# Last LayerNorm by column halves on two engines, fewer products held back, and a re-planned instruction order in a fused attention and gated-MLP kernel

## The chip, the cores and the metric

The kernel runs on one core of a Trainium2 chip. The time is device microseconds (us) from the start to the end of one execution. Engines: TensorE (PE, with its weight loads as PEld), VectorE (DVE), ScalarE (ACT), GpSimd (POOL) and SyncE (SP, which issues most of the DMAs). They run in parallel; each takes its own instructions in the order in which the program lists them, and semaphores hold an instruction until what it needs from another engine is there.

## The reference

A pre-LayerNorm block on x of 2048 rows and 512 columns, bf16:

```python
h  = x + attention(layernorm(x), wqkv, wo)           # 32 heads of 16, softmax over 2048 keys
h2 = h + mlp(layernorm(h), w_gate, w_up, w_down)     # (sigmoid(h @ w_gate) * (h @ w_up)) @ w_down, F = 1792
```

The reference returns h2.

## The kernel before

**Attention.** Scores are computed transposed: a unit is one head's 128 keys by 512 query columns (or 256 columns of two heads). Three units form a tile `pss` in PSUM; there are 683 tiles and two such buffers (`ps_s`, bufs=2), so the scores of tile n wait until tile n-2 has been read. `scores` (its matmuls are at L1119) works in four row strips of PE. For each tile ACT takes the exp of three units (1536 columns) or of two (1024 columns) at L1503. Where it takes two, DVE makes the exp of the third by integer arithmetic: `dexp_first` (L1298) writes J, and after up to four units have been gathered `dexp_rest` adds three shifted copies, the codes (L1318, 512 to 2048 columns by the number of units gathered). `av` (L1272) multiplies the probabilities, J and codes by the values and adds to one accumulator `acc`, in four column strips of PE that run side by side. `finish_group` transposes and normalises the accumulator (L1205, L1167, L1171) and writes the transposed output `ot` (L1183).

**Background work.** Projections, the LayerNorm of earlier row blocks, and the gated MLP (`ffn_up`, `ffn_down`) are generators in a queue `bg`; their matmuls (L214) are taken between score tiles. The rows are treated in eight blocks of 256; the MLP of the first seven runs in the background, that of the last one after the attention.

**The order.** At build time a planner walks through the program with a clock for each engine (`T`), a price for each operation, and picks the next instruction of the engine whose clock is lowest: `pe_step`, `act_step`, `dve_step`, `gps_step`. Prices are constants: `MM` 217.5 ns for a round of products of 512 columns, `SMM` 214 for a score tile, `S_OUT` and `S_IN` (L691) for changing PE from scores to other work and back. Due times spread the background work. Where PE has nothing to do, `fill` (L712) issues a product whose result nobody reads. `MARKS` holds one letter for each tile and engine that bends the rules at that tile: for PE it loosens the room in front of the next scores, favours background work or value products; for ACT it forbids or favours giving a unit to DVE and picks which one; for DVE it moves codes and other work before or behind J. The planner fixes the order alone; at run time only semaphores hold the engines.

**The end.** `ffn_down` of block 6 has two row tiles i of seven steps each (two of the 14 products over f at a time). Steps with f >= `FHOLD` (L1027) of the first, and all of the second, are held back (`HOLD`); the steps that aren't held go to PE before the last value products. Held steps are issued by `release(n)` (L1607), n steps at a time, between the pieces of the last block's work: two of them ahead of the last output projection (L1620, p = 3, which waits for the last `ot`), seven behind it, and the rest after the transposes. The first row tile's steps run in four column strips (L214), the second's over the whole array (L209, into `acc`). The last block's h is gathered in two PSUM tiles `hps[0]`, `hps[1]` of 128 rows and 512 columns; DVE takes the statistics (L187, L190), ACT the root (L1630), DVE the reciprocal and the scaled mean `nmr` (L1631, L1632). Then DVE normalises `hps[0]` (L1636) while ACT normalises `hps[1]` (L1638), PE transposes both (L205), DVE copies the first transpose to `hnT` (L1645), ACT the second (L1643), and the gate and up products of the last block start (L209, `gu`), 112 matmuls of 256 columns.

Of the kernel before, what the change touches and what calls it, by code (L numbers as in the profile page):

```python
# [23 lines left out]
CODE_STEP = (55, 93, 24)  # L24
MARKS = {
    "A": (
        ".....xjj.jo..xoxxooo.oo.jjoj.x.o..x..xooo.....xx.....ooo....jj.......l...j.x"
        "..oloooooooox..jj..jjjjjox..xxxxoxjlooojoj...x.lllll.ll..jx...ljooo.jjl.ll.."
        "x...ll.jj..............jjllll..j..oxll.jl...lllj.j........x.oooljj..jjjjl..."
        "jjjjj.jjjj.j..xxx.o..lllj.jjjjjjxxjj.......x.ll..l...o.x......x..o.oo...l.lo"  # L30
        "ooooooo.....lll...xo.o.oo.o.l.......olll.lox....l..x.j..l....ox.l.l........o"
        "..xjl.........jjl.jj.j...oj...xo..ooo...ool..joool..xlllloo.o.o.l.llol...jj."
        "o..oo...llll.j.l.lxl.oj.xxjjj..lll.....x.....xx....jjl.ll.jjj..ojj.....o...x"
        "x......l.......ooooo.lljljx.oj....xll.....jj.j.jj..j.jjjj.llllxl.jl..jjoo..."
        ".......oooooooojjo.xxoo.jj.jjjjj.l..ox.ll...j.l........ojjj.jjjjo.oo.x.x..."
    ),
    "P": (
        ".......ff...vRR.ww........vww..p..a..RRR....p......v.a.vaafffa.wpa....a...ww"
        "wwwwwfvvaa.vpppp.vv.R.RfR.brrRr....rr.p.....ffffff.rrrr..rrpR.p....aa.a.aaav"
        "pb...RR.b.b..b.b.p...R......vrRrRw.pp.vv....vRfvrpp...........bbRR.Rva.vvr.f"  # L40
        "f.rr.......vvv....fpbr.vvvvvv.v..rpf........r.r..bb...wpww.bb.ppaaw.pRR..pf."
        "....fpp.prR.......R.ffww.pb..v..p.f......vrrrrv..www.v.v..f....vvvvvvbRR..aw"
        "wwwff.ff...vv..p............wva...wwwfRrbbvb......p........r..fvvvpva.r...aa"
        "....pv.....wpppp...p.r...vpv............aw.bbww..w...f..f.ppp.......R.R.aa.b"
        "b.f.rrrrrrrv...rw.w.www..p....a..a...aav....ff...ffr.aa....rppv.ffff.bf....."
        "vv..r....a.Rvvv.vvp.pbb.R.v.v......r........RRv..rr..rfff..a..a...vv...frrr"
    ),
    "D": (
        "...e.e...........cc....cc...ee..........c......ce.c..........c..c..........."
        ".c..s.ssssseee.e..ceeeee.ees..sseee........e.eeeeee.cee.........s..........."  # L50
        "...sc.s........c.e.....s...........ccsssss.ss...ss...........c.cc.ccc......."
        ".....c.ccscc..eee........e.c.c.........c..eee..c.ccc..ceeeeee..c.....c.....e"
        "ee.ee..c.c........e.e.....c.cc....................ece.s..............ce.scc."
        ".s......c......e.cce......c.e.e.c.ccc.e.....c.c.c.e.ee.ce...cc......c......."
        "......ccc...cccc..c....e.............ee......e...............c.......s......"
        "c............cessss..eeecc....eee.ees.e........s.s................s.c......."
        "....scccc...e.......c.......ee.c..........e.......c..ccccccs...sse.....c..."
    ),
}

# [1 line left out]
def kernel(  # L62
# [625 lines left out]
                        moved = True  # L688

    MM = 217.5  # L690
    SMM, S_OUT, S_IN = 214.0, 113.0, 97.0  # L691
    FILL = 2000.0
    SPAN = 3413.0
    FROOM = 200
# [329 lines left out]
        yield pe(0, st["pm"])  # L1024

    HOLD = Mark(None)
    FHOLD = 6  # L1027
    LEAD = 12
    FFN_DUE = (220, 295, 371, 446, 521, 597, 672)
    bg = deque()  # L1030
# [366 lines left out]
    def pe_step():  # L1397
        nonlocal credit
        t, s, e = T["P"], nxt["s"], nxt["e"]
        ready = None  # L1400
        if s < N and (s < 2 or s - 2 in ex_end):
            ready = max(ex_end.get(s - 2, -LAT) + LAT, arrived(s))
            if ready <= t + 100 * (st["mode"] != "s") + 20:
                scores(s)
                nxt["s"] += 1
                for q, p, kt, j in tiles[s]:
                    if (q, kt, j) == (NQC + NH - 1, NT - 1, 3):
                        for g in range(2 * p * (p > 1), min(2 * p + 2, FC // 2)):
# [48 lines left out]
    def act_step():  # L1457
# [59 lines left out]
    def dve_step():  # L1517
# [97 lines left out]

    for p in range(NP):
        if p == NP - 1:
            release(2)
        for i in range(HT):
            nc.tensor.matmul(hps[i], lhsT=OT[hf, p][:, i * P:(i + 1) * P], rhs=wo_sb[:, p, :],  # L1620
                             start=False, stop=(p == NP - 1))
# [6 lines left out]
    for i in range(HT):  # L1628
# [2 lines left out]
    nc.vector.reciprocal(out=rstd[:], in_=rstd[:])  # L1631
    nc.vector.scalar_tensor_tensor(out=nmr[:], in0=mv[:, :, 0], scalar=-1.0, in1=rstd[:],  # L1632
                                   op0=ALU.mult, op1=ALU.mult)
    release(7)
    hnl = [ptp.tile([P, GU, QC], BF16, name="pt")[:, 0, :] for i in range(HT)]
    nc.vector.tensor_scalar(out=hnl[0], in0=hps[0], scalar1=mv[:, 0, 0:1], scalar2=rstd[:, 0:1],  # L1636
                            op0=ALU.subtract, op1=ALU.mult)
    nc.scalar.activation(out=hnl[1], in_=hps[1], func=ACT.Identity, bias=nmr[:, 1:2],  # L1638
                         scale=rstd[:, 1:2])
    for i in range(HT):  # L1640
        pt = transpose4(gu[i], hnl[i])
        if i % 2:
            nc.scalar.copy(out=hnT[:, :, i * P:(i + 1) * P], in_=pt)  # L1643
        else:
            nc.vector.tensor_copy(out=hnT[:, :, i * P:(i + 1) * P], in_=pt)  # L1645
    release(len(bg) * FC)
    for job in held:
        job.fn()
# [54 lines left out]
```

## Time and profile before

| | us |
|---|---|
| median of 3 runs (782.69 to 783.16) | 783.05 |
| the profiled execution, own time | 784.36 |
| its span (first to last instruction) | 782.6 |
| exps (ACT, L1503) from | 21.35 |
| last exp ends | 752.51 |
| last block's gate products start | 760.80 |

PE is busy for 756.3 us of the span, ACT for 753.4, DVE for 728.6. Busy times of ACT count an instruction from when the engine took it up, so neighbours overlap; a group's mean can therefore be longer than the distance of two starts. PE's matmuls are pipelined in the same way. In a row of a group stand: line, engine, operation, output and input with shapes, count, busy time in us and mean in ns, idle time before and what ended it. In a row in order of time: start in us, length in us, the same names, the count of merged instructions, and in brackets the idle time before with what ended it. In a row of a stage: the stretch, its length, the busy time and count of each engine, the granted PE clock as a share, DMA.

### The profile page before, as it was taken

What the parts mean: (1) busy time and instruction counts of PE and PEld (TensorE: products, weight loads), DVE (VectorE), ACT (ScalarE), POOL (GpSimd) and SP (SyncE); (2) the same over time, 40 slices, a digit from 0 to 9 for tenths busy, and PEclk for the clock granted to TensorE, in tenths of its full rate; (3) what the DMA queues carried; (4) which work ended last, traced back from release to release, by engine and by line L of the source; (5) the groups of instructions that cost most, each with busy time, mean ns of one, the idle gap of its engine ahead of it and who ended that gap; (6) DMA issues with size and microseconds to landing.
All of it is one profiled execution on the core that took longest, in us unless ns stands there. A gap on an engine that the chain in (4) does not pass through costs nothing.

```text
span 782.6 us, 34120 instructions
## 1 busy us (share of the span) xinstructions
PE 756.3 (97%) x15312; PEld 374.1 (48%) x15312; DVE 728.6 (93%) x1351; ACT 753.4 (96%) x786; POOL 50.1 (6%) x124
## 2 busy tenths in 40 slices
PE   8899999999999999999999999999999999999998
PEld 7433323444455534554455434654554345544656
DVE  6999998999999999999999999999999999999952
ACT  6999999999999999999999999999999999999972
POOL 2000000000020001000100002000100010001000
PEclk9999999999999999999999999999999999999999
DMA  6403013146012320222022401221132203214510
GB/s 200 122 2 76 2 28 69 30 97 183 9 37 70 97 57 16 77 84 57 9 64 75 115 26 30 85 84 37 37 97 83 64 24 109 84 29 124 167 33 22
DMA packets 93811, 53.00 MB, mean 68 GB/s; under 512 B 21520, under 2 KB 92576, under 8 KB 93664
## 3 DMA queue, kind: packets, MB, share of 16 engines
q1 hardware_dynamic: 92848, 50.56, 23.4%
q8 instruction: 119, 1.95, 1.0%
q10 hardware_dynamic: 816, 0.26, 0.1%
q14 instruction: 28, 0.23, 0.1%
HBM read 39.52 MB, written 2.11 MB: 53 GB/s over the span
## 4 chain that ended last, share of the span: by engine, by line
PE 39%; ACT 32%; DVE 15%; issue 11%; DMA 1%; SPq 1%; POOL 0%; ACTq 0%; DVEq 0%
ACT pt L1503 31%; PE pm L214 12%; PE acc L1272 11%; PE pss L1119 11%; DVE J L1298 7%; DVE code L1318 5%; PE gu L209 2%; ACT th L983 1%; DMA code<-in_A_x_dram 1%; DVE qd L815 1%; PE hp L1673 1%; DVE hT L967 1%; DVE xs L1205 0%; PE acc L209 0%; DVE h L932 0%
## 5 line engine op out<-in xcount | busy, mean ns | idle before, releaser
L1503 ACT ACTIVATE pt<-pss 128x1024 bf16<-128x1024 f32 (+1 forms) x683 | 713.3, 1199 | 3.1 <-PE pss L1119 2.1
L1298 DVE TENSOR_SCALAR J<-pss 128x512 uint16<-128x512 f32 x507 | 337.8, 683 | 12.2 <-PE pss L1119 10.3
L1119 PE MATMUL pss<-QT,KT 32*128 32x256 bf16 (+1 forms) x3584 | 269.4, 288 | 18.6 <-ACT pt L1503 12.3
L1318 DVE TENSOR_SCALAR code<-J 128x2048 uint16<-128x2048 uint16 (+3 forms) x405 | 254.3, 662 | 0.6
L1272 PE MATMUL acc<-pt,Vaug 128*17 128x256 bf16 (+1 forms) x2689 | 229.8, 290 | 0.0
L1272 PE MATMUL acc<-code,Vaug 128*17 128x256 bf16 (+1 forms) x2685 | 199.7, 288 | 0.2
L1119 PEld LDWEIGHTS <-KT 32*128 32x128 bf16 x3584 | 87.5, 92 | 212.4 <-issue 114.1
L1272 PEld LDWEIGHTS <-Vaug 128*17 128x17 bf16 x6269 | 138.9, 90 | 102.1 <-issue 82.8
L1272 PE MATMUL acc<-J,Vaug 128*17 128x256 bf16 (+1 forms) x895 | 141.8, 288 | 0.0
L214 PE MATMUL pm<-xT,wgu 128*32 128x256 bf16 x3136 | 117.0, 274 | 0.3 <-DVE hT L967 0.2
L214 PEld LDWEIGHTS <-wgu 128*32 128x32 bf16 x3136 | 77.3, 96 | 25.2 <-issue 23.0
L214 PE MATMUL pm<-wd,hT 128*32 128x512 bf16 x728 | 54.0, 383 | 0.0
L1171 POOL TENSOR_TENSOR o<-xs,rec 128x256 bf16<-128x256 f32 x23 | 16.5, 719 | 381.7 <-DVE rec L1167 381.7
L967 DVE SCALAR_TENSOR_TENSOR hT<-th,pm 128x512 bf16<-128x512 f32 x49 | 33.3, 679 | 6.2 <-PE pm L214 3.4
L983 ACT ACTIVATE th<-pm 128x512 f32<-128x512 f32 x49 | 31.9, 651 | 0.0
L1205 DVE STREAM_TRANSPOSE xs<-acc 128x512 f32<-128x512 f32 x32 | 22.7, 710 | 5.3 <-PE acc L1272 5.1
L214 PEld LDWEIGHTS <-hT 128*32 128x32 bf16 x728 | 14.5, 95 | 17.0 <-issue 13.2
L214 PE MATMUL pm<-xT,wk_sb 128*32 128x512 bf16 x256 | 19.9, 383 | 0.0
L214 PE MATMUL pm<-xT,wq_sb 128*32 128x512 bf16 x256 | 19.1, 383 | 0.0
L214 PE MATMUL pm<-wv_sb,xT 128*32 128x448 bf16 x256 | 18.0, 356 | 0.0
L1177 POOL TENSOR_TENSOR o<-xs,rec 128x256 bf16<-128x256 f32 x8 | 5.6, 703 | 186.5 <-DVE rec L1167 186.5
L214 PE MATMUL pm<-wo_sb,ot 128*32 128x512 bf16 x224 | 17.4, 383 | 0.0
(155 smaller groups left out, 351.8 us busy)
## 6 DMA issues: line engine op xcount, KB each, us to landing
wgu<-in_B_w_gate_dram SPq DMA_DIRECT2D x49, 256.0 KB
wgu<-in_B_w_up_dram SPq DMA_DIRECT2D x49, 256.0 KB
KT<-half_neg SPq DMA_DIRECT2D x7, 512.0 KB
QT<-qd SPq DMA_DIRECT2D x28, 128.0 KB
KT<-kd SPq DMA_DIRECT2D x7, 256.0 KB
wd<-in_B_w_down_dram SPq DMA_DIRECT2D x1, 1792.0 KB
xr<-in_A_x_dram SPq DMA_DIRECT2D x14, 128.0 KB
out_dram<-ob SPq DMA_DIRECT2D x14, 128.0 KB
```

The costliest lines, as they stand in the source:

```text
L209: nc.tensor.matmul(ps, lhsT=lhsT, rhs=rhs, start=start, stop=stop)
L214: nc.tensor.matmul(ps[r, :], lhsT=lhsT[:, r], rhs=rhs, start=start, stop=stop, tile_position=(0, 32 * j), skip_group_check=True)
L815: nc.vector.tensor_tensor(out=qd[:, 0], in0=ps, in1=RQ[:] if qc else RK[:, 0], op=ALU.mult)
L967: nc.vector.scalar_tensor_tensor(out=hT[:, 2 * k:2 * k + 2, :].rearrange("p f q -> p (f q)"), in0=th[:], scalar=1.0, in1=ps, op0=ALU.add, ...
L983: nc.scalar.activation(out=th[:], in_=ps, func=ACT.Tanh, scale=0.5)
L1119: mm = nc.tensor.matmul(pss[:, ui, a * w:(a + 1) * w], lhsT=KT[hg[a]][32 * j:32 * j + 32, kt * P:(kt + 1) * P], rhs=(QT0[q] if q < NQC and ...
L1171: V.tensor_tensor(out=o2[:, 0:NB, :].rearrange("p b (a d) -> p a b d", a=2), in0=xs[:, :, 0:DH].rearrange("p (a b) d -> p a b d", a=2), in ...
L1205: j = st["acc"] = dve(630, lambda: nc.vector.transpose(out=xs[:].rearrange("p b r -> p (b r)"), in_=acc[:]), Mark(T["P"] + 175))
L1272: nc.tensor.matmul(acc[32 * j:32 * j + VW, a * w:(a + 1) * w], lhsT=Vaug[:, kt, 4 * hg[a] + j, :], rhs=un.ap[:, a * w:(a + 1) * w], start= ...
L1298: first = nc.vector.tensor_scalar(out=J[:, k, :], in0=src, scalar1=128 * SC * LOG2E, scalar2=float(CODE_BASE), op0=ALU.mult, op1=ALU.add)
L1318: nc.vector.tensor_scalar(out=c, in0=j, scalar1=CODE_STEP[i], scalar2=None, op0=ALU.add)
L1503: ex = nc.scalar.activation(out=pt[:, lo:lo + wa, :], in_=pss[:, lo:lo + wa, :], func=ACT.Exp, scale=SC)
```

## The change

Planner: the prices `S_OUT` and `S_IN` grow; six new letters for marks are understood (and two digits), and all three mark strings are replaced, so the order of all engines' instructions changes through the attention. End: `FHOLD` grows from 6 to 12, so that three more steps of the first row tile go ahead of the last value products; one held step instead of two stands ahead of the last output projection; six instead of seven behind it, now issued after the normalisation's instructions. Each of the two row tiles is normalised in halves, columns 0 to 255 on DVE and 256 to 511 on ACT; the second transpose is copied by ACT and DVE in halves.

```diff
 MARKS = {
     "A": (
-        ".....xjj.jo..xoxxooo.oo.jjoj.x.o..x..xooo.....xx.....ooo....jj.......l...j.x"
+        ".....xxj.jo..xoxxoo..oo.jjoj.uoo..ll.xooo.....xx.....oo.ooooo..t......o..j.o"
...
-    SMM, S_OUT, S_IN = 214.0, 113.0, 97.0
+    SMM, S_OUT, S_IN = 214.0, 116.5, 106.5
...
-    FHOLD = 6
+    FHOLD = 12
...
-        room = limit - t + {"w": 150, "v": -150}.get(way, 0)
-        got = [av_ready(60.0, r) for r in (1, 2, 3, 4)]
+        room = limit - t + {"w": 150, "v": -150, "W": 400}.get(way, 0)
+        got = [av_ready(60.0, r) for r in range(1, {"1": 2, "2": 3}.get(way, 5))]
...
-            if kind == "b" and (2 * MM + S_OUT * (st["mode"] == "s") <= room + (0 if credit < 8 else 500)):
+            if kind == "b" and way != "n" and (2 * MM + S_OUT * (st["mode"] == "s") <= room + (0 if credit < 8 else 500)):
...
-        if job and (start is None or job.ready() <= start + 100):
+        if job and (start is None or job.ready() <= start + {"t": 600, "u": -300}.get(mark("A", n), 100)):
...
-        if jq and sc_end[jq[0][0]] + LAT <= t + WAITJ and (half or len(first_codes) < NJB):
+        if jq and sc_end[jq[0][0]] + LAT <= t + {"w": 700, "z": 0}.get(mark("D", nxt["e"]), WAITJ) and (half or len(first_codes) < NJB):
...
         if p == NP - 1:
-            release(2)
+            release(1)
...
-    release(7)
     hnl = [ptp.tile([P, GU, QC], BF16, name="pt")[:, 0, :] for i in range(HT)]
-    nc.vector.tensor_scalar(out=hnl[0], in0=hps[0], scalar1=mv[:, 0, 0:1], scalar2=rstd[:, 0:1],
-                            op0=ALU.subtract, op1=ALU.mult)
-    nc.scalar.activation(out=hnl[1], in_=hps[1], func=ACT.Identity, bias=nmr[:, 1:2],
-                         scale=rstd[:, 1:2])
     for i in range(HT):
-        pt = transpose4(gu[i], hnl[i])
-        if i % 2:
-            nc.scalar.copy(out=hnT[:, :, i * P:(i + 1) * P], in_=pt)
-        else:
-            nc.vector.tensor_copy(out=hnT[:, :, i * P:(i + 1) * P], in_=pt)
+        nc.vector.tensor_scalar(out=hnl[i][:, 0:HQ], in0=hps[i][:, 0:HQ], scalar1=mv[:, i, 0:1],
+                                scalar2=rstd[:, i:i + 1], op0=ALU.subtract, op1=ALU.mult)
+        nc.scalar.activation(out=hnl[i][:, HQ:D], in_=hps[i][:, HQ:D], func=ACT.Identity,
+                             bias=nmr[:, i:i + 1], scale=rstd[:, i:i + 1])
+    release(6)
+    pts = [transpose4(gu[i], hnl[i]) for i in range(HT)]
+    nc.vector.tensor_copy(out=hnT[:, :, 0:P], in_=pts[0])
+    nc.scalar.copy(out=hnT[:, 0:2, P:2 * P], in_=pts[1][:, 0:2, :])
+    nc.vector.tensor_copy(out=hnT[:, 2:4, P:2 * P], in_=pts[1][:, 2:4, :])
     release(len(bg) * FC)
```

More of the change, by code (lines that the diff above doesn't have):

```diff
@@ L26 @@
     "A": (
-        ".....xjj.jo..xoxxooo.oo.jjoj.x.o..x..xooo.....xx.....ooo....jj.......l...j.x"
[L28 to L32, printed above, removed]
@@ L33 @@
-        "o..oo...llll.j.l.lxl.oj.xxjjj..lll.....x.....xx....jjl.ll.jjj..ojj.....o...x"
-        "x......l.......ooooo.lljljx.oj....xll.....jj.j.jj..j.jjjj.llllxl.jl..jjoo..."
-        ".......oooooooojjo.xxoo.jj.jjjjj.l..ox.ll...j.l........ojjj.jjjjo.oo.x.x..."
+        ".....xxj.jo..xoxxoo..oo.jjoj.uoo..ll.xooo.....xx.....oo.ooooo..t......o..j.o"
+        "..o...oooooox..jj...j........lxxxx.......j...xtll........jxo..xuooooojl.ll.."
+        "x...ll.jj.............jjj.joo..j.......jl...lllj.j........x..oojjjjjj.jjlul."
@@ new lines @@
+        "jjjjjljjjt.j..xxxoo..luuj.jjj.j...j...j....ju.uujo...o.x..u...x..o.oo...uulo"
+        "...oooo.....uul........oo.o.o....u..olll.lox....llll.j.......o..l.l.l...llll"
+        "..xol....t....jjl.jj.j...oj...xo..oxo...otlll.ll.l..xl.llouj..loolluu.uu.u.u"
+        "o..oo...llll.j.l.jooo.....jjj..llt.tjj.j......xuuujuu.u.l.j..jjj.j.jj..o...x"
+        "xuuuu..u..xx...ooooo.lljlj..xj....xll.....jj.jljj.jjjjjjj.lllllloooo.jjoo..."
+        "j..t.ttt.ooooo.jjouuuu......jjjj.l..oxloo...j.l........ojjj.jj.......x.xtt."
@@ L36 @@
     ),
     "P": (
[L38 to L43, printed above, removed]
@@ L44 @@
-        "....pv.....wpppp...p.r...vpv............aw.bbww..w...f..f.ppp.......R.R.aa.b"
-        "b.f.rrrrrrrv...rw.w.www..p....a..a...aav....ff...ffr.aa....rppv.ffff.bf....."
-        "vv..r....a.Rvvv.vvp.pbb.R.v.v......r........RRv..rr..rfff..a..a...vv...frrr"
+        ".......ff.11vRR.11..W.....vww.WWW.W.wwwwv.W.WWW1W....n.vaaf.fa.w.aaa..a.WWWW"
+        ".w.1111v.a.vrrr.rrrrWW.W..brrpr.....r.p.b...ffff1..ffw.ff...22bb.b.aappppaav"
+        "pb...RR.b.b..b.b.p.........bvrRrrw.pp.vv....vRfvwwp22222222r..b1R........Rp2"
@@ new lines @@
+        "2.22.....v.vvvw...fpbr.vvvRR.RRr.11rrr.nn.nnnnr..bppppprfp.ba.p.app.wwww..aa"
+        "....fp..prR.....f.R.ffww.pb.ava...22.....vvrrrv....1...aawRa.apv1vvvvbRR.r22"
+        "22222.ff...wv........v....n.wva...wwwfRrpbvb....2.p........rRnfvvbbna.r....."
+        ".vvv.v.v...wpbpp...p.r....pvWW.ffR.vRRRRf.1......2rr.r..f....p.......1......"
+        "b...rrwwr......r2.222222.p....n.nR.b.....2p.f.fvvvvr.aa...WWWW..f1....f....."
+        "pW.2.2.pp.ppaaaarvp.pb..R.v.v......r..2R....RRv..vr..rfff..a..a........frrr"
@@ L47 @@
     ),
     "D": (
[L49 to L54, printed above, removed]
@@ L55 @@
-        "......ccc...cccc..c....e.............ee......e...............c.......s......"
-        "c............cessss..eeecc....eee.ees.e........s.s................s.c......."
-        "....scccc...e.......c.......ee.c..........e.......c..ccccccs...sse.....c..."
+        "...e.e..wwww.........s.cc...ee..........c......sssss.........c..c.....eeww.."
+        "cc.cs.ssssseeees..ceeeee.eezzzc..c.........e.eeecce.cee.........s..........."
+        "...sc.s........c.e.....s..ss.s.....ccsssss.ss..ess.......e...c.zc.ccc......."
@@ new lines @@
+        ".....c.ccs....eee........e.c.eeeeeeee..c..eee..c.ccc..css...e..c.ww......w.e"
+        ".w.ee..c.c........e.e.....c.......................ecee.eee.e....ss...ce.scc."
+        ".s.c....w..w...e.cce...c..c.e.e.c.ccese...cc..c.c.e.ee.cw...c.......c......."
+        "....z.ceee..cccc..s....ee............ee...ss.ww.w............c..zzzzzz......"
+        "w............cessss..eeecc....eew....sw........s.s......ww........s.c..ee..."
+        "....scccc..ce.......c......ccccc..........e.......c..ccccccs...sse.....c..."
```

## The prediction

> **What bounds the kernel now.** I read the page first, then the groups by form, then stages, then single rows in order of time.
>
> ```profile
> span 782.6 us, 34120 instructions
> PE 756.3 (97%) x15312; PEld 374.1 (48%) x15312; DVE 728.6 (93%) x1351; ACT 753.4 (96%) x786; POOL 50.1 (6%) x124
> PE 39%; ACT 32%; DVE 15%; issue 11%; DMA 1%; SPq 1%; POOL 0%; ACTq 0%; DVEq 0%
> ```
>
> Three engines are over 90% busy, and the chain that ended last (third row) passes between them: no single one owns the span. Which of them sets the pace has to be read from prices. These are the groups by form, then single rows of ACT in order of time (start, length):
>
> ```profile
> L1503 ACT ACTIVATE pt<-pss 128x1024 bf16<-128x1024 f32 x508 | 495.3, 1092 | 3.0 <-PE pss L1119 2.1 <-ACT pt L1503 0.3
> L1503 ACT ACTIVATE pt<-pss 128x1536 bf16<-128x1536 f32 x175 | 253.6, 1512 | 0.1
> L983 ACT ACTIVATE th<-pm 128x512 f32<-128x512 f32 x49 | 31.9, 651 | 0.0
> ```
> ```profile
> 21.35 1.94 ACT L1503 ACTIVATE pt<-pss 128x1024 bf16<-128x1024 f32 x2 [0.94 <-PE pss L1119]
> ...
> 35.26 1.44 ACT L1503 ACTIVATE pt<-pss 128x1536 bf16<-128x1536 f32 x1
> 39.25 1.48 ACT L1503 ACTIVATE pt<-pss 128x1536 bf16<-128x1536 f32 x1
> 47.29 1.14 ACT L1503 ACTIVATE pt<-pss 128x1024 bf16<-128x1024 f32 x1
> 51.81 1.21 ACT L1503 ACTIVATE pt<-pss 128x1024 bf16<-128x1024 f32 x1
> ...
> 748.28 0.63 ACT L983 ACTIVATE th<-pm 128x512 f32<-128x512 f32 x1
> 748.77 3.74 ACT L1503 ACTIVATE pt<-pss 128x1536 bf16<-128x1536 f32 x3
> ```
>
> The means (1092 and 1512 ns) are no prices: they overlap their neighbours. The price is the distance of starts in an unbroken run. From 35.26 to 39.25 lie three exps of 1536 columns, 1.33 us each; from 47.29 to 51.81 five of 1024, 0.904 each; a tanh takes 0.49 (748.28 to 748.77). Then ACT's work is 508 x 0.904 + 175 x 1.33 + 49 x 0.49 = 459.2 + 232.8 + 24.0 = 716.0 us. It runs from 21.35 to 752.51 (748.77 + 3.74), 731.2 us. So ACT loses only **15.2 us** in the whole attention stage. A stage cannot get shorter than ACT's work; these 15.2 us are all that a better order can win there.
>
> ```profile
> 21.35:752.50 731.15, 712.38 (x14836) 340.81 (x14837) 703.34 (x1262) 728.94 (x732) 44.53 (x102) 1.00 0.24 66
> 752.50:760.80 8.30, 8.30 (x82) 3.53 (x73) 5.29 (x13) 3.24 (x7) 0.00 (x0) 1.00 0.08 22
> 760.80:782.60 21.80, 18.46 (x155) 14.96 (x153) 5.97 (x10) 6.74 (x12) 0.00 (x0) 0.98 0.08 26
> ```
>
> In this view of stages the columns are length, PE, PEld, DVE, ACT, POOL busy, granted clock. PE is busy for 97% of the first stage at full clock and DVE for 96%: ACT's lost time is scores that came late because PE or DVE was late. The second stage is the last LayerNorm and its neighbours; the third (the last gate, up and down products) keeps its instructions.
>
> **The change part by part.** *The attention stage.* The planner's numbers and marks change the order everywhere, so I count in the built programs. Scores stand in 668 separate blocks in both, so the number of switches into and out of scores stays. On ACT 506 exps of 1024 and 177 of 1536 replace 508 and 175: two units go from DVE to ACT, 2 x (1.33 - 0.904) = **+0.85 us** on the engine with the least slack. PE loses work:
>
> ```profile
> 760.80 12.39 PE L209 MATMUL gu<-xT,KT 128*128 128x256 bf16 x112
> ```
> ```profile
> L712 PE MATMUL pm<-xT 128*32 128x512 bf16 x28 | 10.8, 386 | 0.1
> L1298 DVE TENSOR_SCALAR J<-pss 128x512 uint16<-128x512 f32 x507 | 337.8, 683 | 12.2 <-PE pss L1119 10.3
> L1318 DVE TENSOR_SCALAR code<-J 128x2048 uint16<-128x2048 uint16 x360 | 239.5, 695 | 0.5
> L1318 DVE TENSOR_SCALAR code<-J 128x1536 uint16<-128x1536 uint16 x12 | 6.3, 558 | 0.0
> L1318 DVE TENSOR_SCALAR code<-J 128x512 uint16<-128x512 uint16 x21 | 4.9, 295 | 0.0
> L1318 DVE TENSOR_SCALAR code<-J 128x1024 uint16<-128x1024 uint16 x12 | 4.5, 428 | 0.0
> ```
>
> A product of 256 columns takes 12.39 / 112 = 0.11 us, one of 512 0.22. Fillers (L712) go from 28 to 23. The probability-times-value products run in four column strips side by side; adding the longest strip of every block gives 962 products of 512 before and 951 after. Together 16 x 0.22 = **3.5 us** less on PE. On DVE, J goes from 507 to 505, and codes of 2048, 1536, 1024 and 512 columns from 360, 12, 12, 21 to 354, 18, 18, 9: -1.4 - 4.2 + 3.3 + 2.6 - 3.5 = -3.2 us.
>
> What that is worth is not in any row, since it depends on where the late scores are. Bounds: at best all 15.2 us of ACT's loss go; at worst the new order makes scores later than now, and I allow 3 us. A nearer estimate on the low side: over every six successive tiles, PE's slots (products at the prices above, 0.21 for a switch, the row below) exceed ACT's in 186 places before and in 130 after, and the summed excess, divided by six since each tile lies in six such stretches, falls from 6.7 to 4.6 us, so 2.1. The switch:
>
> ```profile
> 750.88 0.22 PEld L1272 LDWEIGHTS <-Vaug 128*17 128x17 bf16 x9 [0.21 <-issue]
> ```
>
> I take **-3.5 us**: PE's cut one for one, because its idle time in this stage (731.15 - 712.38) hardly exceeds ACT's, so the two wait for each other in turn, and DVE is relieved by as much.
>
> *After the last scores.* PE's rows, with ACT's and DVE's:
>
> ```profile
> 750.56 0.39 PE L1119 MATMUL pss<-QT,KT 32*128 32x256 bf16 x4
> 751.29 1.28 PE L214 MATMUL pm<-wd,hT 128*32 128x512 bf16 x20
> 752.57 0.49 PE L1272 MATMUL acc<-pt,Vaug 128*17 128x256 bf16 x9
> ...
> 754.59 0.45 DVE L1183 STREAM_TRANSPOSE ot<-o 128x256 bf16<-128x256 bf16 x1
> 754.82 1.05 PE L214 MATMUL pm<-wd,hT 128*32 128x512 bf16 x16
> 755.80 0.61 PE L1620 MATMUL hp<-wo_sb,ot 128*128 128x512 bf16 x2
> ...
> 758.37 0.16 DVE L1632 SCALAR_TENSOR_TENSOR nmr<-mv,rstd 128x2 f32<-128x2 f32 x1
> 758.44 0.80 DVE L1636 TENSOR_SCALAR pt<-hp,mv,rstd 128x512 bf16<-128x512 f32 x1
> 758.62 0.78 ACT L1638 ACTIVATE pt<-hp,nmr,rstd 128x512 bf16<-128x512 f32 x1 [0.49 <-DVE nmr L1632]
> 759.49 0.61 PE L205 MATMUL gu<-ident_bf,pt 128*128 128x128 bf16 x8
> 759.91 0.42 DVE L1645 COPY xT<-gu 128x512 bf16<-128x512 bf16 x1 [0.66 <-PE gu L205]
> ```
>
> Keeping fewer products (FHOLD 12) puts 48 down products, not 24, between the last scores and the last probability-times-value products. Before, these 24 end just as ACT's last exp does (752.51), so PE has no slack there. Four run side by side: 24 more are 6 x 0.22 = **+1.3 us** on the path to OT's last transpose and everything behind it. All other PE work of that gap is equal (22 value products).
>
> Ahead of the last output projection stand 8 down products instead of 16: 2 x 0.22 = **-0.44**. The transpose is done at 755.04 (754.59 + 0.45) and PE is free at 755.36, so PE still sets it and the whole gain counts. Statistics up to nmr then follow at the same distance. Behind them 12 whole products (2.6 us) fill PE from 755.8 to 758.4, ahead of the normalised rows: fillers no longer hold up the transposes.
>
> *The halves.* In the built program's waits, ACT's half of each row tile waits for DVE's half of the same tile, and DVE's copy of half the second transpose waits for ACT's copy. So the pairs run one after another. From nmr's end (758.53 before) I reckon with these rows:
>
> ```profile
> L1665 DVE SCALAR_TENSOR_TENSOR ob<-gu,pt 128x256 bf16<-128x256 f32 x1 | 0.4, 425 | 5.3 <-PE gu L1673 5.3
> L1650 ACT ACTIVATE pt<-hp 128x256 f32<-128x256 f32 x1 | 0.4, 390 | 0.0
> L365 DVE TENSOR_TENSOR qn<-qn 128x256 bf16<-128x256 bf16 x3 | 0.9, 284 | 0.0
> ```
>
> DVE's halves end at 0.42 and 0.78; ACT's run from 0.51 (0.09 behind DVE, as 758.62 is behind 758.53) to 0.90 and from 0.87 to 1.26. The second tile's transposes start at 1.33, are readable 0.42 later (759.49 to 759.91), ACT copies half until 2.16, DVE the rest until 2.48. The gate product needs that part only from its third step on, so it starts as if at 2.34; before it started at 760.80, 2.27 behind nmr: **+0.07**. The nearest rows bound this from 0.5 less (side by side, below) to 0.3 more (all four steps wait).
>
> The PSUM page of the Trainium skill ("PSUM — Partial Sum Buffer", section "PSUM bank collisions raise a hardware error") says that two engines on one bank and quadrant collide, reads against reads included, and must be guarded by bank. It speaks against halving a tile between two engines: by it those waits cannot go, and the sum is the one above; without it the halves would be worth 0.5 us. No run here shows two engines on one such tile; on two tiles they do work side by side (758.44 and 758.62).
>
> The sum: 784.36 (own time of the profiled execution, 782.6 of span and 1.76 around it) + 0.85 - 3.5 + 1.3 - 0.44 + 0.07 = 782.64. That execution is 1.31 over the median of 783.05, so I forecast **781.3 us**.
>
> **The rivals.**
>
> *The cut misses (slower).* PE's shed work lay where ACT did not wait, so ACT's 15.2 us stay; what remains is the two units on ACT and the 24 products behind the last scores: 0.85 + 0.93 = +1.8, **784.8 us**. For it: fillers go where PE has nothing else to do. It decides from the point where the loss falls by less than 0.2 us. If the loss grows by up to 3 us it is 787.8.
>
> *Little of it lands.* The six-tile count holds, -2.1: **782.7 us**, down to -0.3, 784.5: within 0.2%.
>
> *The account was the fault (faster).* The planner reckoned 113 + 97 ns for a switch out of and into scores and now 223: 13 ns x 667 = 8.7 us of PE time that the old order did not foresee. If that is why scores are late, the loss halves, -7.6: **777.2 us**; at two thirds of that, 779.7. Against it: PE's idle time stands beside ACT's, so an early score absorbs many of the 13 ns.
>
> *The halves do run side by side.* If a wait is met earlier than I read it, the gate product starts 1.77 behind nmr, not 2.34: **780.7 us**.
>
> **How the numbers follow.** Measurement of this kernel cannot tell less than about 0.2% (1.6 us) from no change. Forecast (780.3 to 782.4): 0.40, of which 0.24 under 781.5. Cut misses: 0.20, slower. Little lands: 0.19, same. Account: 0.17, faster. Side by side: 0.04, faster. So faster 0.24 + 0.17 + 0.04 = 0.45, same 0.16 + 0.19 = 0.35, slower 0.20. The range 778.0 to 785.4 leaves out about 0.1 on either side.
>
> **What would show it.** 506 and 177 exps, and ACT's loss (by the same three prices) near 11.7 us; from the last scores to the first gate product 11.2 us, where 10.24 are now; the last value products over 1 us after the last exp's end; the last two output projection products about 0.4 sooner behind the transpose; ACT's halves starting only after DVE's end. I am wrong if ACT's loss stays near 15 us, or if the last value products follow the last exp at once.

## The result, and the profile after

The changed kernel takes **786.83 us** (median of 6 runs, 786.64 to 787.98), the kernel before in the same session 783.43 (782.69 to 784.47): **0.5% slower**, ratio 1.0049 [1.0038, 1.0059]. I had forecast 781.3, faster, in a range of 778.0 to 785.4. The time lies in the rival "the cut misses", between its 784.8 and 787.8. The profiled execution has 786.73 us of its own, 784.9 of them span. Two of the experiments, e2_no_fill and e4_after_shift5, had a disturbed profiled execution; their times are used, their traces not.

The page of the changed kernel, the same three rows as before (span, busy time by engine, chain by engine):

```profile
span 784.9 us, 34074 instructions
PE 753.7 (96%) x15289; PEld 373.7 (48%) x15292; DVE 726.5 (93%) x1345; ACT 754.4 (96%) x787; POOL 45.3 (6%) x124
PE 35%; ACT 33%; DVE 19%; issue 11%; DMA 1%; SPq 0%; POOL 0%; ACTq 0%; DVEq 0%
```

PE and DVE have less to do, ACT 1 us more, and the span is longer. The groups by form show the planned units, 506 and 177:

```profile
L1503 ACT ACTIVATE pt<-pss 128x1024 bf16<-128x1024 f32 x506 | 492.0, 1103 | 2.1 <-PE pss L1119 1.2
L1503 ACT ACTIVATE pt<-pss 128x1536 bf16<-128x1536 f32 x177 | 255.6, 1517 | 0.8 <-PE acc L1272 0.4 <-PE pss L1119 0.2
```

Now the stages (length, then busy time of PE, PEld, DVE, ACT, POOL, granted clock): first exp to last exp's end, from there to the third step of the gate product, and the rest. The changed kernel:

```profile
20.95:753.47 732.52, 710.53 (x14818) 341.17 (x14821) 701.03 (x1255) 729.95 (x732) 39.69 (x102) 1.00 0.24 66
753.47:763.10 9.63, 8.70 (x80) 3.73 (x74) 5.36 (x15) 3.66 (x9) 0.00 (x0) 1.00 0.06 17
763.10:784.90 21.80, 18.19 (x152) 14.76 (x151) 6.38 (x10) 6.45 (x11) 0.00 (x0) 1.00 0.08 25
```

and the attention stage of the kernel before in a second profile, taken beside the first experiments:

```profile
20.60:750.82 730.22, 711.31 (x14835) 341.01 (x14837) 703.27 (x1263) 728.83 (x732) 44.56 (x102) 1.00 0.24 66
```

The second profile was needed: in the one on which the prediction rests, ACT waited 0.93 us once at the third exp (its first row of exps merges two, 21.35 for 1.94; the new trace starts with four in a row). Against 730.22 the attention is **2.3 us longer**. ACT's work by the prediction's three prices went from 716.0 to 506 x 0.904 + 177 x 1.33 + 49 x 0.49 = 716.84 us, so its loss went from 14.2 to **15.7 us**, where the prediction has 11.7. PE's busy time in the stage fell by only 0.8 (711.31 to 710.53), where the prediction's count of its products has 3.5, and its idle time rose from 18.9 (730.22 - 711.31) to 22.0: PE waited more than before.

The end of the changed kernel in order of time (start, length):

```profile
751.35 0.39 PE L1119 MATMUL pss<-QT,KT 32*128 32x256 bf16 x4
751.89 2.76 PE L214 MATMUL pm<-wd,hT 128*32 128x512 bf16 x48
754.60 0.49 PE L1272 MATMUL acc<-pt,Vaug 128*17 128x256 bf16 x7
756.64 0.45 DVE L1183 STREAM_TRANSPOSE ot<-o 128x256 bf16<-128x256 bf16 x1
756.86 0.62 PE L214 MATMUL pm<-wd,hT 128*32 128x512 bf16 x8
757.40 0.60 PE L1620 MATMUL hp<-wo_sb,ot 128*128 128x512 bf16 x2
...
759.97 0.16 DVE L1632 SCALAR_TENSOR_TENSOR nmr<-mv,rstd 128x2 f32<-128x2 f32 x1
760.04 0.99 DVE L1636 TENSOR_SCALAR pt<-hp,mv,rstd 128x256 bf16<-128x256 f32 x2
760.68 0.56 ACT L1638 ACTIVATE pt<-hp,nmr,rstd 128x256 bf16<-128x256 f32 x1 [0.94 <-DVE pt L1636]
761.40 0.57 ACT L1638 ACTIVATE pt<-hp,nmr,rstd 128x256 bf16<-128x256 f32 x1 [0.16 <-ACT pt L1638]
761.62 0.42 DVE L1642 COPY xT<-gu 128x512 bf16<-128x512 bf16 x1 [0.59 <-PE gu L205]
762.35 0.37 ACT L1643 COPY xT<-gu 128x256 bf16<-128x256 bf16 x1 [0.38 <-PE gu L205]
762.75 0.29 DVE L1644 COPY xT<-gu 128x256 bf16<-128x256 bf16 x1 [0.71 <-ACT xT L1643]
762.77 12.49 PE L209 MATMUL gu<-xT,KT 128*128 128x256 bf16 x112
```

48 down products stand between the last scores and the last value products; the seven of these that are shown start 1.1 us behind the last exp's end (754.60 - 753.47). The last projection follows its transpose by 0.31 (757.40 - 757.09), by 0.76 before. ACT's first half starts only when DVE's is done (idle 0.94; before, waiting for nmr alone, 0.49). From nmr's end (760.13) to the gate product are 2.64 us, 2.27 before. From the last scores to it 11.4 us; forecast 11.2, before 10.24.

Summed between the two fast-starting traces: attention +2.3 (ACT's work +0.85, its loss +1.5), products behind the last scores +1.07 (last exp's end to the first product into `hps[1]`: 0.71 before, 1.78 after), release -0.43, nmr to gate +0.37, third gate step +0.1. That is **+3.4 us**, which is the result.

### The profile page after: what moved, and what is told of

Read it like the earlier page. It is cut to its first block, busy times and chain, and to the rows that moved or that the text cites. A ratio compares the mean times of both kernels' runs of the same rounds, so it can differ in the third digit from the quotient of the medians.

```text
span 784.9 us, 34074 instructions
## 1 busy us (share of the span) xinstructions
PE 753.7 (96%) x15289; PEld 373.7 (48%) x15292; DVE 726.5 (93%) x1345; ACT 754.4 (96%) x787; POOL 45.3 (6%) x124
## 4 chain that ended last, share of the span: by engine, by line
PE 35%; ACT 33%; DVE 19%; issue 11%; DMA 1%; SPq 0%; POOL 0%; ACTq 0%; DVEq 0%
ACT pt L1503 31%; PE pm L214 11%; PE pss L1119 10%; PE acc L1272 10%; DVE J L1298 8%; DVE code L1318 5%; PE gu L209 2%; ACT th L983 2%; DVE hT L967 1%; DVE xs L1205 1%; PE hp L1672 1%; DMA code<-in_A_x_dram 1%; DVE st L187 0%; DVE xT L944 0%; DVE xT L958 0%
## 5 line engine op out<-in xcount | busy, mean ns | idle before, releaser
L1318 DVE TENSOR_SCALAR code<-J 128x2048 uint16<-128x2048 uint16 (+3 forms) x399 | 251.5, 662 | 0.4
L1272 PE MATMUL acc<-code,Vaug 128*17 128x256 bf16 (+1 forms) x2670 | 194.4, 288 | 0.1
L1119 PEld LDWEIGHTS <-KT 32*128 32x128 bf16 x3584 | 90.5, 92 | 213.6 <-issue 111.8
L1272 PEld LDWEIGHTS <-Vaug 128*17 128x17 bf16 x6254 | 136.3, 90 | 99.1 <-issue 79.3
L214 PE MATMUL pm<-xT,wgu 128*32 128x256 bf16 x3136 | 115.1, 274 | 0.7
L214 PEld LDWEIGHTS <-wgu 128*32 128x32 bf16 x3136 | 75.6, 96 | 26.7 <-issue 24.9
```

Source lines behind the costliest of these rows:

```text
L214: nc.tensor.matmul(ps[r, :], lhsT=lhsT[:, r], rhs=rhs, start=start, stop=stop, tile_position=(0, 32 * j), skip_group_check=True)
L1119: mm = nc.tensor.matmul(pss[:, ui, a * w:(a + 1) * w], lhsT=KT[hg[a]][32 * j:32 * j + 32, kt * P:(kt + 1) * P], rhs=(QT0[q] if q < NQC and ...
L1272: nc.tensor.matmul(acc[32 * j:32 * j + VW, a * w:(a + 1) * w], lhsT=Vaug[:, kt, 4 * hg[a] + j, :], rhs=un.ap[:, a * w:(a + 1) * w], start= ...
L1318: nc.vector.tensor_scalar(out=c, in0=j, scalar1=CODE_STEP[i], scalar2=None, op0=ALU.add)
```

## The experiments

"Loss" is ACT's loss in the attention by the same prices; "tail" the part behind the last exp.

**1. Which part costs?** Both kernels again, and each part alone: the tail on the old order, and the new order with the old tail.

```diff
# e1_new_tail is before with this and the halves; e1_old_tail is after with the reverse of it
-    FHOLD = 6
+    FHOLD = 12
-            release(2)
+            release(1)
-    release(7)
+    release(6)
```

> The kernel before, unchanged, for a second profile. All theories: ratio 1.000 (within 0.2%). ACT's idle time in the attention stage was 15.2 us in the first profile; if it comes out within 0.5 us of that, differences of 1 us between two orders can be read from one profile each; if it differs by 2 us or more, they cannot.

> The changed kernel, unchanged, on this chip. All theories: +3.4 us (+0.3 to +0.6%). ACT's idle time near 15.7 us, as in its first profile; the last value products end about 1.1 us later behind the last exp than in the kernel before.

> The kernel before with its old marks and prices, and the end of the changed kernel (FHOLD 12, one and six steps released, halves). The exps, units and fillers are those of before. Theory 'both': the end costs +1.1 us (24 products behind the last scores +1.1, release ahead of the output projection -0.4, halves +0.4 to +0.5), so 784.5. Rival 'the order alone': 0, 783.4. Rival 'the end alone': the whole +3.4, 786.8.

> The changed kernel with its new marks and prices, and the end of the kernel before (FHOLD 6, two and seven steps released, whole row tiles). Theory 'both': the new order keeps its cost, +1.4 us read from the two profiles and up to +2.3 by the medians, so 784.8 to 785.7. Rival 'the order alone': +3.4, 786.8. Rival 'the end alone': 0, 783.4.

Against the kernel before: before again 1.0002 [0.9994, 1.0011], after again 787.39 us, 1.0058 [1.0045, 1.007], new tail 784.09, 1.0016 [1.0007, 1.0025], old tail 786.31, 1.0043 [1.003, 1.0055]. Both parts cost, the order more: by the traces a third of the lost time is the tail (1.1 of 3.4 us) and two thirds the order, by the ratios about a quarter and three quarters. ACT's loss repeats within 0.1 us for one program (changed kernel 15.68 and 15.75; old order with either tail 14.23 and 14.25), but for the one wait at the third exp: it makes the 1.0 by which the first profile of the kernel before is higher. So the loss is a property of the order, not chance.

**2. Is the loss PE's?** In e2_no_fill the 28 fillers are not issued (nothing reads them). In e2_half_down every second down product in the background is left out, so the MLP's output lacks them.

```diff
-            nc.tensor.matmul(ps[0:32, :], lhsT=src[:, 0, 0:32], rhs=rhs, ...)      # e2_no_fill
-        for f in range(a, b):                                                       # e2_half_down
+        for f in range(a, b, (skip := 2 if mm is quarters else 1)):
...
-    SMM, S_OUT, S_IN = 214.0, 113.0, 97.0                                           # e2_prices_only
+    SMM, S_OUT, S_IN = 214.0, 116.5, 106.5
```

> The kernel before with the planner unchanged, but its 28 filler products (L712, whose results nobody reads) are not issued: every other instruction stands in the same order, PE has 28 x 0.22 = 6.2 us less work. Theory 'only the blocks that stand ahead of a late score count': fillers stand where PE would wait, so ACT's idle time stays within 0.7 us of 14.5 and the time within 1 us of 783. Rival 'PE's cut counts one for one' (the step of the prediction): ACT's idle time falls to about 8 us, 777.

> The kernel before, but every second product of the background down projections is left out (the output lacks half of the MLP's sum in seven of the eight row blocks): same plan, about 18 us less PE work in the attention stage, in blocks that do stand ahead of scores. Theory 'only the blocks ahead of a late score count': ACT's idle time falls by no more than the share of late scores that follow down products, 1 to 4 us, and another 0.5 to 1 us is saved behind the last scores: 778 to 782. Rival 'one for one': ACT's idle time goes to nearly nothing, -13 us and the end's 1 us: 769.

> The kernel before with the two new switch prices and its old marks. The built program takes 497 exps of 1024 columns and 186 of 1536, 40 fillers. Theory 'ACT's work is the floor and idle time comes on top': 11 units more on ACT are 11 x 0.426 = +4.7 us; marks made for another plan leave ACT's idle time no lower than 14.5, so 788 or more. Rival 'the old account caused the idle time': the idle time falls by 5 us or more with the truer prices, so 783 or less.

Without fillers 783.48 us, 1.0006 [0.9996, 1.0016]: nothing gained. With half the down products 782.77, 0.999 [0.998, 0.9999] (778 to 782 expected). Its attention stage:

```profile
21.39:751.00 729.61, 699.33 (x14490) 340.59 (x14489) 702.68 (x1263) 727.66 (x732) 43.21 (x102) 1.00 0.24 66
```

PE is busy 12 us less than in 711.31 (by the prediction's price the 345 missing products are 345 / 4 x 0.22 = 19 us), and the stage is 0.6 shorter (1.4 without a single wait of 0.74 at the third exp, which this execution has and the other hasn't). One microsecond off PE's busy time is worth about a tenth off ACT's loss. Where it goes show the waits (engine and line, what it waited for: us in total, times, longest), first of the kernel before, then of e2_half_down:

```profile
PEld L1119 <- DVE J L1298: 48.9, 148, 0.9
PE pss L1119 <- ACT pt L1503: 12.9, 44, 0.6
PE pss L1119 <- DVE J L1298: 1.9, 6, 0.6
```
```profile
PEld L1119 <- DVE J L1298: 53.6, 167, 0.9
PE pss L1119 <- ACT pt L1503: 22.2, 80, 0.6
PE pss L1119 <- DVE J L1298: 2.3, 7, 0.6
```

With less to do PE stands longer in front of the scores. The weight loads (PEld) overlap other products, so their 48.9 us are not idle time of PE; PE's own waits in these rows are mostly for ACT's exp. To see which read frees a tile last, set the start of each tile's scores against the ends of the exp and of J on tile n-2. In the kernel before PE stands idle for 18.1 us in front of scores (88 tiles, counting gaps from 0.02 us, shorter ones than the rows): in 16.0 of them ACT's exp ends last, in 2.1 DVE's J. In e2_half_down it is 29.0, of which 26.3 for the exp. Those scores come no sooner, since the exp ends no sooner, and they cost ACT little (0.5 us behind the exp, 0.8 behind J).

ACT loses at other tiles: 11.1 of its 14.2 us fall on 88 exps whose scores start over 0.15 us behind both reads, while PE is still at other products. Only work that stands there is worth taking out. Down products are PE's last work ahead of 1.3 of the 11.1 us, and with half of them left out 10.0 remain.

The prices alone, with the old marks, gave 796.05, 1.016 [1.0144, 1.0176]: 497 exps of 1024 and 186 of 1536 (ACT's work +4.7), loss +3.4, and 4.5 us more behind the last exp, where up products now stand behind the last scores, ahead of the down products. The old marks were made for the old prices; the new prices give no better order by themselves.

**3. What do ACT's work and the marks give?** e3_more_act adds 25 exps of 512 columns, whose results nobody reads. e3_after_half_down takes half the down products from the changed kernel, with the same lack in its output. e3_hybrid76 has the new prices and marks for the first 76 tiles, which ended 0.7 us sooner in the changed kernel (79.66 us behind the first exp instead of 80.35), then the old ones and the old tail.

```diff
...
+        if split and st["extra"] > 0:                                   # e3_more_act, 25 times
+            nc.scalar.activation(out=pt[:, 0 if lo else GU - 1, :], in_=xTf[3][:, 0:QC], func=ACT.Exp, scale=SC)
+    SMM, prices = 214.0, lambda: (116.5, 106.5) if nxt["s"] < 76 else (113.0, 97.0)   # e3_hybrid76
```

> The kernel before with 25 exps of 512 columns added on ACT, spread over the attention stage, whose results nobody reads; the order of all else is the same. Theory 'ACT's work is the floor, its idle time comes from single late scores': 25 x 0.48 (a tanh of 512 columns takes 0.49) = +12 us, of which idle time behind some of them takes back at most 2: +10 to +12, 793 to 795. Rival 'PE or DVE set the pace and ACT waits for them': up to the 14.5 us of ACT's idle time hide it, 0 to +3, under 786.

> The changed kernel with every second product of the background down projections left out (as in the earlier run of the kernel before, where ACT's idle time fell by 1.5 us and the time by 0.7 us, for 18 us less on PE). Theory 'the new order's extra 1.5 us of ACT's idle time are late scores behind single blocks of background work': idle falls by 2 to 3 us. Rival 'they are late reads by DVE or blocks of value products': idle falls by 1 to 1.5 us as before. The time behind the last exp falls by 1 us in both.

> The new marks and prices for the first 76 tiles, the old ones from there, and the end of the kernel before. The built program has 509 exps of 1024 and 174 of 1536. Theory 'ACT's work plus single late scores': the first 76 tiles take 79.7 us instead of 80.4, ACT's work falls by 0.43 us, and where the later order comes out as before the rest is equal: -0.3 to -1.2 us, 782.2. Rival 'marks only fit the plan that they were made with': ACT's idle time in the later tiles grows by over 1 us, 784 or more.

More ACT work: 794.12, 1.0135 [1.0121, 1.0149]. The 25 exps take 0.52 us each (start to start), 13.0 in sum, and the stage grew from 730.22 by

```profile
21.40:762.35 740.95, 713.06 (x14838) 343.11 (x14837) 705.57 (x1263) 740.18 (x757) 43.56 (x102) 1.00 0.24 65
```

10.7 us: work added to ACT costs eight tenths of its length, while work taken off PE gives back one tenth. Half down products out of the changed kernel: 784.76, 1.0015 [1.0006, 1.0024], its loss 0.9 lower (1 to 3 expected) for 13 us off PE: again under a tenth, so taking work off PE at large would not mend the new order. The hybrid: 784.03, 1.0004 [0.9996, 1.0013] (782.2 expected); the first 76 tiles do end at 79.66, and that is lost at the seam, where the loss of the second 76 tiles is 2.8 instead of 1.5.

**4. What do the halves cost?** Whole tiles in the changed kernel, and halves crossed: DVE takes the left half of one tile while ACT takes the right half of the other.

```diff
+        k = HT - 1 - i                                        # e3_crossed
-        nc.scalar.activation(out=hnl[i][:, HQ:D], in_=hps[i][:, HQ:D], ...
+        nc.scalar.activation(out=hnl[k][:, HQ:D], in_=hps[k][:, HQ:D], ...
```

> The changed kernel with the row tiles normalised whole, one on each engine, and copied whole, as before; all else as changed. Theory 'the halves run one after another': from nmr to the first gate product 2.0 to 2.3 us instead of 2.64, so 0.4 to 0.6 us faster than the changed kernel, 786.4 where that is 787. Rival 'the halves cost nothing': the same distance within 0.1 us and the same time.

> The changed kernel with ACT's halves taken in the other order: while DVE has the left half of the first row tile, ACT has the right half of the second, then they change over, so no half waits for the other engine on the same tile at the start. Theory 'ACT's halves wait for DVE's on the same tile': ACT starts 0.1 us behind nmr, not 0.55; both tiles are whole at about 1.1 us behind nmr instead of 1.1 and 1.8, and the gate product starts 0.2 to 0.5 us earlier behind nmr than 2.64. Rival 'no wait between the halves': ACT's first half starts as late as before, 2.64.

Whole tiles 785.96, 1.0036 [1.0024, 1.0048]; crossed 786.37, 1.0033 [1.002, 1.0047], both lower than the changed kernel's 1.0049 and 1.0058, though the intervals touch; it is the rows that carry it. Those of e2_whole_tiles:

```profile
759.63 0.16 DVE L1632 SCALAR_TENSOR_TENSOR nmr<-mv,rstd 128x2 f32<-128x2 f32 x1
759.71 0.80 DVE L1635 TENSOR_SCALAR pt<-hp,mv,rstd 128x512 bf16<-128x512 f32 x1
759.88 0.78 ACT L1637 ACTIVATE pt<-hp,nmr,rstd 128x512 bf16<-128x512 f32 x1 [0.49 <-DVE nmr L1632]
761.23 0.59 ACT L1643 COPY xT<-gu 128x512 bf16<-128x512 bf16 x1 [0.56 <-PE gu L205]
761.86 1.36 PE L209 MATMUL gu<-xT,KT 128*128 128x256 bf16 x11 [0.24 <-ACT xT L1643]
```

The gate product comes 2.07 behind nmr's end; with halves 2.64, crossed 2.15. A half on ACT takes 0.56 us where a whole tile takes 0.78: halving the columns saves 0.22, not 0.39. Two halves on ACT and the wait for DVE are longer than one whole tile beside DVE's. In the crossed kernel ACT's first half starts 0.09 behind nmr instead of 0.55. The PSUM page of the Trainium skill, section "PSUM bank collisions raise a hardware error", says that two engines must not be on one bank and quadrant at once. The waits agree with it (in the changed kernel ACT stands idle for 0.94 us until DVE's half of the same tile is done); halves of the same tile on both engines at once stay untried.

**5. Why do some exps start late?** In the traces a waiting exp mostly starts 0.50 us behind the first score product of its tile, but some 0.775 behind. I numbered ACT's instructions in the built programs. In the eighteen traces that are used none at the places 60, 188, 316, ... (each 128th, counted with its semaphore instructions; 128 exps in all) starts under 0.774; others go down to 0.50, a few to 0.44. Before, these are tiles 12, 140, 321, 443 and 505; after, 12, 76, 141, 324, 445, 565 and 624, and **ACT's second half of the normalisation**, at place 1468. Five one-column instructions ahead of the attention move all places and keep all else.

```diff
     nc.scalar.activation(out=small.tile([P, 1], FP32, name="warm")[:], in_=eps_t[:], func=ACT.Sqrt)
+    for _ in range(5): nc.scalar.activation(out=small.tile([P, 1], FP32, name="warm")[:], in_=eps_t[:], func=ACT.Sqrt)
```

Twenty instead of five in e4_after_shift20, eighteen in e5_before_shift18; e4_release_shift5 is the kernel before with the five and `release(1)` in place of `release(2)`.

> The changed kernel with five more one-column ACT instructions ahead of the attention; nothing else differs, the attention's instructions are the same ones in the same order on every engine, only the place of each in ACT's stream moves by five. Theory 'every 64th': a waiting ACT instruction at places 60, 124, 188, ... of its stream starts 0.275 us later behind what it waits for than another; in the trace of the changed kernel seven waiting exps (tiles 12, 76, 141, 324, 445, 565, 624) and ACT's second half of the normalisation stand there, with five more none does. By the idle time ahead of each (0.10 to 0.63 us, at most 0.275 of each) ACT's idle time in the attention falls by 1.5 us, the second half comes 0.26 sooner: 1.5 to 1.8 us faster than the changed kernel, 785.0 to 785.5, and no waiting exp starts 0.77 behind its first score product. Rival 'order': these late starts come from what the plan makes wait, the place in the stream has nothing to do with it: 787 as before, the same tiles start 0.77 behind.

> The changed kernel with five more one-column ACT instructions once more, for a trace that nothing disturbed. By the theory of every 128th instruction the seven late exps of the changed kernel start 0.50 to 0.70 behind their first score product, 1.3 us less in sum; ACT's idle time in the attention falls from 16.0 to about 14.7, ACT's second half ends 0.27 sooner: 785.5. By 'order' 787.

> The changed kernel with twenty more one-column ACT instructions ahead of the attention. Theory 'every 64th': the late places now fall on four waiting exps, tiles 34, 436, 465 and 586 (idle ahead of them 0.15, 0.13, 0.18, 0.05 us so far, each to grow to about 0.3 to 0.45), and on none of the seven, and not on the second half: 0.275 each, 1.1 us more than with five added, so 0.4 to 0.7 us faster than the changed kernel, if the twenty themselves are hidden at the start (they come while ACT waits for the first loads). Rival 'order': no change, the same seven tiles late.

> The kernel before with five more one-column ACT instructions ahead of the attention. Theory 'every 64th': five waiting exps (tiles 12, 140, 321, 443, 505) leave the late places and no other waiting exp takes them: ACT's idle time falls by 0.9 us, 782.0 to 782.6 where the kernel before has 783.2. Then the places explain 0.6 of the 1.5 us of idle time by which the two kernels differ (0.9 of the tail's and the attention's 3.5), and changed and before with five added differ by 2.6. Rival 'order': 783.2.

> The kernel before with eighteen more one-column ACT instructions ahead of the attention. The traces so far say more narrowly: it is every 128th instruction of ACT's stream (places 60, 188, 316, ...), and an exp there never starts less than 0.774 us behind its first score product, while others start down to 0.497. By this theory the late places fall on tiles 67, 131, 195, 253, 313, 435 and 555, which so far start 0.50, 0.55, 0.50, 0.55, 0.61, 0.68 and 0.50 behind: each goes to 0.775, 1.53 us in sum, against 0.91 in the kernel before and 0.16 with five added. So 0.6 us slower than the kernel before (783.7 where it has 783.1) and 1.4 slower than with five added. Rival 'order': 783.1, and the tiles 12, 140, 321, 443, 505 late. Rival 'more instructions at the start move something else': these seven tiles not at 0.775.

> The kernel before with the one part of the change that gained, release of one kept product instead of two ahead of the last output projection, and the five ACT instructions. The first gives 0.43 us by the stage behind the last exp (2.15 instead of 2.58 from the first step to the last projection), the second 0.9 by the theory 'every 64th': 781.6 to 782.2, 0.2% faster than the kernel before. By 'order' 782.8.

The changed kernel with five: 785.66, 1.0031 [1.0019, 1.0043], and again 785.54, 1.0036 [1.0023, 1.0048], against 1.0058 without. Tile 565 in the changed kernel, then with five added (e5_after_shift5_again):

```profile
623.69 0.39 PE L1119 MATMUL pss<-QT,KT 32*128 32x256 bf16 x6
624.47 1.02 ACT L1503 ACTIVATE pt<-pss 128x1024 bf16<-128x1024 f32 x1 [0.51 <-PE pss L1119]
```
```profile
623.18 0.39 PE L1119 MATMUL pss<-QT,KT 32*128 32x256 bf16 x6
623.68 1.02 ACT L1503 ACTIVATE pt<-pss 128x1024 bf16<-128x1024 f32 x1 [0.24 <-PE pss L1119]
```

The same instructions, and ACT waits 0.24 instead of 0.51. All seven came sooner; the loss fell by 1.0 (1.3 to 1.5 expected), nmr to gate from 2.64 to 2.37. With twenty 785.91, 1.0034 [1.0021, 1.0047]: the seven and the second half came sooner, but of the four tiles that I had named only 436 was late, with 66, 131, 195, 555 and 615. I had taken each 64th place and only exps that waited already; it is each 128th, and one that would start less than 0.775 behind its scores without having waited is late too. By this corrected rule I named seven tiles for e5_before_shift18 ahead of the run, and all seven (67, 131, 195, 253, 313, 435, 555) came at 0.774 to 0.792; the five old ones at 0.497 to 0.657. Times of the kernel before with five and with eighteen: 782.25, 0.9992 [0.9983, 1.0001], and 783.44, 1.0007 [0.9998, 1.0016]. They lie 1.2 us apart (1.4 expected); either interval alone holds 1, so it is the tiles' starts that carry the verdict. With five the loss of the kernel before fell by 0.6 (0.9 expected): the five late tiles came sooner, but tile 621 took such a place and went from 0.626 to 0.778.

So the place explains 0.4 us of the attention's 2.3 (with five added to both kernels the stages are 731.52 and 729.62, 1.9 apart), and 0.27 of the tail's 1.1. From the first exp to the last store the traces then differ by 2.7 us instead of 3.4. The rest belongs to the order: ACT's 0.85 and 1.1 of loss.

The page "Runtime: NRT & Kernel Launch" of the Trainium skill, section "Instruction fetch mechanics", says that an engine's instructions are fetched in blocks of 256 and that crossing a block's border is mostly hidden. The runs show a period of 128, hidden where ACT is behind its work, and about 0.28 us (0.774 less 0.50) where it waits. Whether fetching is the cause no run shows.

e4_release_shift5, meant to beat both kernels, gave 782.61, 0.9993 [0.9984, 1.0002]: not faster than the five alone. Its rows show why:

```profile
757.05 0.16 DVE L1632 SCALAR_TENSOR_TENSOR nmr<-mv,rstd 128x2 f32<-128x2 f32 x1
758.61 1.46 PE L209 MATMUL acc<-wd,hT 128*128 128x512 bf16 x6
758.81 0.59 ACT L1643 COPY xT<-gu 128x512 bf16<-128x512 bf16 x1 [0.73 <-PE gu L205]
759.91 3.33 PE L209 MATMUL gu<-xT,KT 128*128 128x256 bf16 x29
```

The projection came 0.43 sooner, but the step of two products that is not released ahead of it now stands behind the transposes, six instead of four, and they hold the gate product until 759.91, half a microsecond after the copy (759.40). Nmr to gate is 2.70 instead of 2.27: given back to the last hundredth. In the changed kernel the 0.43 is real only because 24 products were moved ahead of the last value products, for 1.07.

## Why the prediction was wrong

- **ACT's two units, +0.85: right.** 506 and 177 came as counted, and by e3_more_act work added to ACT costs eight tenths of its length.
- **Attention -3.5: the step that failed,** "PE's cut one for one". The prediction read 97% busy on PE and nearly equal idle times of PE and ACT as two engines that wait for each other in turn. They do, but at different tiles: PE's idle time stands where ACT's exp of tile n-2 isn't done (16.0 of 18.1 us), ACT's loss where PE is still at other products (11.1 of 14.2). Work taken off PE elsewhere joins PE's wait and doesn't reach ACT's: 12 us off PE gave 1.4, leaving out the fillers nothing. At that rate the cut was worth some 0.4 us at most, while the loss rose by 1.5, 0.4 of it by ACT's places. My six-tile count (-2.1) forecast a fall too; why it failed is not shown. DVE, which it leaves out, can be little of it: J ends last ahead of late exps of 0.8 us before and 0.9 after.
- **24 products, +1.3: right in mechanism, 1.07 measured.** Kept with the release (-0.44, measured -0.43) they are a net cost of 0.64.
- **Halves, +0.07: the waits were right, the price wrong.** 0.48 was measured (0.37 to the gate, 0.1 at its third step). 0.27 is the second half's place in ACT's stream. The half's price came from a copy (0.39) where a scaled and biased half takes 0.56. And whole tiles would have gained 0.2 with fewer products behind the transposes (2.07 instead of 2.27), which the sum did not credit.
- **The rival "the cut misses" held** in its wider form, loss growing; its working (0.85 + 0.93) lacked the loss's 1.5 and 0.41 of the halves' 0.48. "The account was the fault" fell: the larger prices alone cost 12.8 us (796.05 - 783.22).
- Own time less median, 1.31: 0.93 of it was the one wait at the third exp.

Open is why the new marks make the loss larger beyond the places, +1.0: with five added to both, the loss in tiles 380 to 682 is 8.3 us after and 6.0 before, and ahead of them 6.4 and 7.6, but no single mark was shown to be it. Without the five, the part of the loss at scores behind PE's work hardly changed in sum (11.1 us at 88 exps before, 11.2 at 75 after), so the rise lies in the other gaps. No run takes work off DVE alone, so what its time is worth stays open too.

## What to carry to other kernels

Before crediting work taken from a busy engine, look at what that engine waits for at the instruction that others need: if it is another engine's read, the saved time joins the wait. Count only work that stands ahead of the instructions that are late. Price the rate of exchange once on the chip, by taking work out of one engine and putting work into another (here one tenth of what was taken off PE, eight tenths of what was added to ACT). And when instructions are kept back as filling, count them in every place where they can come to stand: moved ahead of one step, they leave the next; not issued there, they block it.

## What was not expected of the hardware

An exp at each 128th place of ACT's stream starts at the earliest 0.774 us behind the first of the score products it waits for, others mostly 0.50, so that a few instructions more far ahead move the time by some 1.2 us in this kernel (782.25 with five added, 783.44 with eighteen). ACT's half of 256 columns costs 0.56 of the 0.78 of 512. And the loss of a given program is the same from run to run within 0.1 us, but for single waits of 0.7 to 1.0 us at the start.
